# The issue order of all five engines and the buffer of each tile, worked out anew for an adaLN block with Hedgehog linear attention and a channel MLP

## The chip, the cores and the metric

The kernel runs on one core of one Trainium2 chip. The metric is the device time of one execution in microseconds, the median of several runs. The engines are named as in the profile: PE multiplies matrices (PEld loads its weights), DVE is the vector engine, ACT the scalar engine, POOL the GpSimd engine, and SP issues the transfers (DMAs).

## The reference

A residual block on x of 2048 rows by 512, all in fp32, with one condition vector c. Six rows of 512 come out of `silu(c) @ w_mod` and modulate the two halves of the block. Cut to what matters:

```python
mod = (_silu(c) @ w_mod).reshape(c.shape[0], 6, 1, -1)      # sa, ca, ga, sb, cb, gb
h = _layernorm(x) * (1 + ca) + sa
q, k, v = split(h @ wqkv)                                    # 32 heads of 16
pq, pk = q @ w_phi, k @ w_phi                                # per head
phi = concat([softmax(p), softmax(-p)])                      # for pq and for pk, 32 features
kv, z = phi_k^T @ v, sum_s phi_k                             # sums over all 2048 rows
o = (phi_q @ kv) / (phi_q @ z + 1e-6)
x = x + ga * (o @ wo)
h = _layernorm(x) * (1 + cb) + sb
y = gelu(_layernorm(h) @ w1 + b1) @ w2 + b2                  # 512 -> 1376 -> 512
x = x + gb * y
```

The sums `kv` and `z` run over all rows, so nothing of the second half can start before the last row of the first half is through.

## The kernel before, in words

The 2048 rows are cut into eight blocks of 256 rows (two tiles of 128). Every large product is made as three fp32r products of high and low parts (`mm3`), so each operand is split first: ACT copies the high part, and DVE or POOL subtracts to get the low part.

The first half (to about 148 us in the profile) works block by block. PE transposes the normalised rows (`hp`), ACT applies the modulation and rounds (`hf`, `hT`), and PE projects to keys (`pk`), values (`pv`) and queries (`pq`). Each key tile then goes through a chain (`k_chain`): DVE takes maximum and minimum (`mxk`), subtracts twice (`ek`), ACT takes the exponential, DVE sums (`smk`) and inverts (`rck`), POOL multiplies, and DVE adds the result to the running sum (`zps`; the last time into `zb`). PE sums the values weighted by the finished key tiles into `pkv`. Beside this the background work (`bg`) prepares the modulation rows (`wms`) and splits weights (`wo`, `w2a`): load, POOL scales, ACT copies, DVE subtracts. At the very start the weights of keys and queries are folded with `w_phi` on PE (`fold`), and the condition is turned into columns: `wm` is loaded, and DVE and POOL multiply it with `scp`.

The two halves meet in `zp`, a product of PE with `zb`, the sum over all key tiles.

The second half works on blocks 0 to 7 again, one ahead of the other: attention of a later block (`attn_ea`: exponentials `eq`, the denominator `dz`, a rearrangement through DRAM `eb`, `et_dram`, `eT`), then `po` (attention output), `oT` (its split), `pw` (times wo), the layer norms (`la`, `lb`, `lc`), a rearrangement of the result (`y`, `yf`; by transposes `yp` on PE for the first two blocks) into `yT`, and the MLP: eleven products `pg` per block (`up`, "u"), each followed by gelu and a copy on ACT (`g`) and a subtraction on DVE, and eleven pairs of products `py` (`down`, "d") that use them.

None of the order is left to a scheduler. The code above is run once to record every operation in a queue under a part (a block), a name and an engine letter (p PE, a ACT, v DVE, g POOL, s SP), and a list called `ISSUE` then says in which order they are issued. All instructions go through one line of the recorder, so the profile shows L194 for everything:

```python
    def issue(self):
        for n, order in enumerate(ISSUE):
            for name in order.split():
                for f in self.queues[n + name.count("+") - name.count("-"), name.strip("+-")].popleft():
                    f()
```

A token such as `-k0.v` takes the next operation of DVE in the key chain of tile 0 of the block before the one that the row stands for. Each engine executes what is issued to it strictly in that order; between engines semaphores hold back what isn't ready. The second table, `SLOTS`, says for a tag of buffers which one each tile gets, and where a tag has no entry the buffers are taken in turn:

```python
    def slot(tag, bufs):
        n = used[tag] = used.get(tag, -1) + 1
        return f"{tag}_{SLOTS[tag][n] if tag in SLOTS else n % bufs}"
```

A tile that takes a buffer still in use waits for the last reader of the tile before it. The tag `mm` has four PSUM banks, through which nearly all products pass.

## Time and profile before

| | |
|---|---|
| median of 3 runs | 496.57 us (496.22 to 496.67) |
| the profiled execution | 496.27 us, of which the span from first to last instruction is 494.2 us |
| mean granted PE clock | 0.995 |
| PE busy | 475.0 us (96% of the span) |
| DVE, ACT, POOL busy | 349.5, 236.4 and 230.8 us |
| moved | 40.42 MB read, 18.88 MB written |

PE is busy almost throughout, so a reader looks first at the few places where it isn't. A busy PE is not PE at its peak, since its pieces overlap and their ends are modelled. Rows of the profile give start, duration or busy time in us, the engine, the operation, the tile written and the tiles read, and in brackets the idle time before it with what ended it.

### The profile page before, as it was taken

What the parts mean: (1) busy time and instruction counts of PE and PEld (TensorE: products, weight loads), DVE (VectorE), ACT (ScalarE), POOL (GpSimd) and SP (SyncE); (2) the same over time, 40 slices, a digit from 0 to 9 for tenths busy, and PEclk for the clock granted to TensorE, in tenths of its full rate; (3) what the DMA queues carried; (4) which work ended last, traced back from release to release, by engine and by line L of the source; (5) the groups of instructions that cost most, each with busy time, mean ns of one, the idle gap of its engine ahead of it and who ended that gap; (6) DMA issues with size and microseconds to landing.
All of it is one profiled execution on the core that took longest, in us unless ns stands there. A gap on an engine that the chain in (4) does not pass through costs nothing. (4 is left out here: it accounts for less than half of the span.)

```text
span 494.2 us, 8537 instructions
## 1 busy us (share of the span) xinstructions
PE 475.0 (96%) x3311; PEld 403.7 (82%) x3311; DVE 349.5 (71%) x662; ACT 236.4 (48%) x439; POOL 230.8 (47%) x175
## 2 busy tenths in 40 slices
PE   4999999899999998999999999999999999999996
PEld 4887877687877785998897998897898998898985
DVE  5998998998996539986986796793785382462311
ACT  3687764546563344547264633842544324134321
POOL 3467875677794684756474534533452210010000
PEclk9999999999999999999999999999999999999999
DMA  8752556542043716116364544507813443202101
GB/s 271 292 170 87 170 192 193 172 127 86 1 129 122 238 42 193 44 38 214 90 171 127 136 123 126 131 1 229 205 37 87 124 132 86 86 1 85 44 0 44
DMA packets 64760, 59.85 MB, mean 121 GB/s; under 512 B 40256, under 2 KB 52176, under 8 KB 64464
## 3 DMA queue, kind: packets, MB, share of 16 engines
q1 hardware_dynamic: 64720, 59.31, 38.8%
q8 instruction: 26, 0.43, 0.3%
q14 instruction: 14, 0.11, 0.1%
HBM read 40.42 MB, written 18.88 MB: 120 GB/s over the span
## 5 line engine op out<-in xcount | busy, mean ns | idle before, releaser
L194 PEld LDWEIGHTS pg<-yT,w 128*128 128x128 f32 x960 | 121.1, 191 | 6.4 <-DVE yT L194 1.0
L194 PE MATMUL pg<-yT,w 128*128 128x256 f32 x960 | 123.2, 283 | 1.5 <-DVE yT L194 0.8
L194 ACT ACTIVATE pg<-pg,blob 128x256 f32<-128x256 f32 (+1 forms) x88 | 39.2, 445 | 99.5 <-PE pg L194 90.9
L194 PE MATMUL py<-w2a,g 128*128 128x512 f32 x288 | 72.7, 392 | 0.0
L194 DVE TENSOR_TENSOR g<-pg,g 128x256 fp32r<-128x256 f32 x80 | 32.3, 412 | 53.8 <-ACT g L194 53.7
L194 PEld LDWEIGHTS py<-w2a,g 128*128 128x128 f32 x288 | 52.0, 189 | 9.9 <-ACT pg L194 0.4
L194 PE MATMUL pv<-wvh,hT 128*128 128x512 f32 x192 | 48.0, 405 | 2.3 <-ACT hf L194 2.0
L194 PE MATMUL pw<-wo,oT 128*128 128x512 f32 x192 | 48.0, 395 | 1.7 <-DVE oT L194 1.0
L194 PE MATMUL py<-w2b,g 128*128 128x512 f32 x192 | 47.9, 394 | 0.0
L194 ACT ACTIVATE g<-pg 128x256 fp32r<-128x256 f32 x80 | 30.7, 384 | 35.3 <-PE py L194 30.4
L194 PE MATMUL pk<-wk,hT 128*128 128x512 f32 x192 | 46.6, 394 | 0.9 <-ACT vf L194 0.9
L194 PE MATMUL pq<-wq,hT 128*128 128x512 f32 x192 | 46.9, 396 | 0.0
L194 POOL TENSOR_TENSOR ez<-eq,zb 128x1024 f32<-128x1024 f32 x15 | 36.2, 2412 | 21.9 <-DVE dz L194 12.4
L194 POOL TENSOR_TENSOR eq<-eq,rcq 128x1024 f32<-128x1024 f32 x15 | 29.9, 2009 | 33.3 <-DVE rcq L194 33.3
L194 PEld LDWEIGHTS pv<-wvh,hT 128*128 128x128 f32 x192 | 36.5, 194 | 10.6 <-ACT hf L194 2.2
L194 PEld LDWEIGHTS pw<-wo,oT 128*128 128x128 f32 x192 | 35.0, 188 | 11.4 <-DVE oT L194 3.4
L194 PEld LDWEIGHTS pk<-wk,hT 128*128 128x128 f32 x192 | 35.4, 188 | 8.5 <-ACT vf L194 1.3
L194 PEld LDWEIGHTS pq<-wq,hT 128*128 128x128 f32 x192 | 35.4, 188 | 8.5 <-issue 0.5
L194 PEld LDWEIGHTS py<-w2b,g 128*128 128x128 f32 x192 | 34.9, 188 | 7.7 <-issue 1.2
L194 POOL TENSOR_TENSOR ek<-ek,rck 128x1024 f32<-128x1024 f32 x16 | 32.5, 2041 | 7.8 <-DVE rck L194 6.6
L194 POOL TENSOR_TENSOR yT<-yf,yT 128x256 fp32r<-128x256 f32 x12 | 9.0, 767 | 44.3 <-ACT yT L194 44.3
L194 DVE TENSOR_REDUCE dz<-ez 128x64 f32<-128x1024 f32 x16 | 19.2, 1198 | 7.8 <-POOL ez L194 7.8
(146 smaller groups left out, 771.2 us busy)
## 6 DMA issues: line engine op xcount, KB each, us to landing
et_dram<-eb SPq DMA_DIRECT2D x48, 128.0 KB, 2.4
eT<-et_dram SPq DMA_DIRECT2D x12, 512.0 KB, 4.2
xt<-in_x SPq DMA_DIRECT2D x8, 512.0 KB, 4.7
wms<-in_wmodT SPq DMA_DIRECT2D x8, 512.0 KB, 3.9
x<-in_x SPq DMA_DIRECT2D x8, 512.0 KB, 4.0
out<-x SPq DMA_DIRECT2D x16, 256.0 KB, 2.0
pq_dram<-qs SPq DMA_DIRECT2D x6, 512.0 KB, 2.9
pq<-pq_dram SPq DMA_DIRECT2D x6, 512.0 KB, 3.7
```

Source lines behind the costliest of these rows:

```text
L194: return lambda *a, **k: self.later.hold(self.letter, lambda: f(*a, **k))
```

## The change

The recorded operations are the same, each with the same shape, on the same engine: 1816 entries in both lists. What is new are the two tables. `ISSUE` lists the entries in another order for all five engines, with more entries moved over a block's border (`+` and `-` before a name), and `SLOTS` names the buffer for every tile of 43 tags, where before it did so for seven and the rest went in turn. No tag has more or fewer buffers. The first lines of the diff:

```diff
 SLOTS = {
-    "acc": "1010101010101010101",
-    "two": "100101",
-    "ek": "010110101010101010101010",
+    "acc": "1010101101001101001",
+    "two": "010110",
+    "xt": "110101010101010101",
+    "st6a": "10001100",
...
 ISSUE = [
     """
-db.s si.a x0.s dk.s dm.s dm.s dm.s dk.s dk.s -init.v si.v si.v bd.v si.v s0.v s0.v s0.v s0.v s0.v -init.v dk.s
+db.s x0.s dk.s dk.s dm.s dm.s dv.s si.a si.v -init.v si.v si.v dm.s sr.p s0.v s0.v dk.s s0.v dq.s -init.v bd.v sr.a
```

Three places of the new order follow. In the changed file the recorder's line is L226 instead of L194.

The first place is the start of the program on SP, the loads. Before (`k` is a quarter of the key weights, `wm` of the first modulation columns, `xt` rows of x):

```order
L194 DMA blob<-in_small 128x217
L194 DMA xt<-in_x 128x2x512
L194 DMA k<-in_wkT 128x512
L194 DMA wm<-in_wmodT 128x1024 x3
L194 DMA k<-in_wkT 128x512 x3
L194 DMA wm<-in_wmodT 128x1024
L194 DMA wv_s<-in_wv 128x1024
```

And now:

```order
L226 DMA blob<-in_small 128x217
L226 DMA xt<-in_x 128x2x512
L226 DMA k<-in_wkT 128x512 x2
L226 DMA wm<-in_wmodT 128x1024 x2
L226 DMA wv_s<-in_wv 128x1024
L226 DMA wm<-in_wmodT 128x1024
L226 DMA k<-in_wkT 128x512
L226 DMA q<-in_wqT 128x1024
L226 DMA wm<-in_wmodT 128x1024
L226 DMA k<-in_wkT 128x512
```

One piece of `k` moved ahead of the first `wm`; the last two pieces of `k` and the last two of `wm` moved back, behind a load of `wv_s` and, for the last of each, one of `q`.

The second place is the end of the first half, on two engines. On DVE, before (the two instructions that write `zb` end the sum that `zp` waits for):

```order
L194 RECIPROCAL rck<-smk 128x64
L194 TENSOR_TENSOR w2a<-ws,w2a 128x1024
L194 TENSOR_TENSOR zps<-zps,ek 128x512
L194 TENSOR_REDUCE mxk<-pk 128x32 x2
L194 TENSOR_TENSOR ek<-pk,mxk 128x32x16
```

Now, with the end of the sum:

```order
L226 RECIPROCAL rck<-smk 128x64
L226 TENSOR_TENSOR zps<-zps,ek 128x512 x4
L226 TENSOR_TENSOR zb<-zps,ek 128x512 x2
L226 TENSOR_TENSOR w2a<-ws,w2a 128x1024
L226 TENSOR_REDUCE dz<-ez 128x64
```

The last subtraction of `w2a`, which stood fifteen rows ahead of the `zb` row, now stands behind it. On PE, around `zp`, before:

```order
L194 MATMUL pq<-wq,hT_330 128x512
L194 MATMUL pkv<-ek,vf 32x64 x32
L194 MATMUL zp<-zb,ones 128x512 x2
L194 MATMUL pq<-wq,hT_329 128x512 x2
L194 MATMUL pq<-wq,hT_330 128x512
L194 MATMUL pq<-wq,hT_329 128x512 x2
L194 MATMUL pq<-wq,hT_330 128x512
L194 MATMUL pq<-wq,hT_329 128x512 x2
L194 MATMUL pq<-wq,hT_330 128x512
L194 MATMUL pq<-wq,hT_329 128x512 x2
L194 MATMUL pq<-wq,hT_330 128x512
L194 MATMUL pkv<-ek,vf 32x64 x32
```

And now:

```order
L226 MATMUL pq<-wq,hT_330 128x512
L226 MATMUL pkv<-ek,vf 32x64 x64
L226 MATMUL zp<-zb,ones 128x512 x2
L226 MATMUL pq<-wq,hT_329 128x512 x2
L226 MATMUL pq<-wq,hT_330 128x512
```

The 32 `pkv` products that came after `zp` now come before it, in one run with the others.

The third place is on PE at the start of the MLP, where the second block's `pw` (`oT_454` and `oT_455` are its operand's high and low part) and the first block's `yp` and `pg` meet. Before:

```order
L194 MATMUL pw<-wo,oT_454 128x512 x2
L194 MATMUL pw<-wo,oT_455 128x512
L194 MATMUL yp<-blob,h_414 128x128 x8
L194 MATMUL pg<-yT_460,w_359 128x256
L194 MATMUL pg<-yT_461,w_359 128x256
```

And now:

```order
L226 MATMUL yp<-blob,h_414 128x128 x8
L226 MATMUL pw<-wo,oT_454 128x512 x2
L226 MATMUL pw<-wo,oT_455 128x512
L226 MATMUL pw<-wo,oT_454 128x512 x2
L226 MATMUL pw<-wo,oT_455 128x512
L226 MATMUL pw<-wo,oT_454 128x512 x2
L226 MATMUL pw<-wo,oT_455 128x512
L226 MATMUL pw<-wo,oT_454 128x512 x2
L226 MATMUL pw<-wo,oT_455 128x512
L226 MATMUL pg<-yT_460,w_359 128x256
```

Twelve `pw` products now stand between the transposes `yp` and the first `pg`, which reads what ACT and DVE make of `yp`; before, `pg` followed `yp` at once.

## Prediction

> **What bounds the kernel now.** I read the page's first part, then busy time by stage, then the waits of PE and of DVE, and last the order of time around the largest waits. The page:

> ```profile
> span 494.2 us, 8537 instructions
> PE 475.0 (96%) x3311; PEld 403.7 (82%) x3311; DVE 349.5 (71%) x662; ACT 236.4 (48%) x439; POOL 230.8 (47%) x175
> ```

> PE leaves 19.2 us of the span unused. The stages show that DVE's 71% is an average over two different halves (columns: stretch, its length, then busy us and instructions of PE, PEld, DVE, ACT, POOL, then the granted clock, DMA share and GB/s):

> ```profile
> 0.00:12.00 12.00, 5.86 (x24) 5.16 (x24) 5.90 (x21) 4.41 (x8) 3.76 (x8) 1.00 0.81 266
> 12.00:148.00 136.00, 131.08 (x1030) 107.00 (x1030) 128.62 (x224) 86.42 (x144) 97.56 (x64) 0.99 0.45 148
> 148.00:330.00 182.00, 179.43 (x1221) 152.26 (x1222) 138.03 (x253) 88.10 (x158) 99.81 (x74) 1.00 0.41 122
> 330.00:494.20 164.20, 158.65 (x1039) 139.28 (x1037) 76.96 (x167) 57.52 (x131) 29.70 (x31) 1.00 0.30 87
> ```

> From 12 to 148 us DVE is busy for 128.6 of 136 us, nearly as much as PE. From 148 us on PE alone bounds: it is busy for 338.1 of 346.2 us. What ends PE's waits (engine, tile, releaser: us in total, times, longest):

> ```profile
> PE scp L194 <- DVE sc L194: 4.1, 1, 4.1
> PE fold L194 <- DMA k<-in_wkT: 2.2, 2, 1.4
> PE pv L194 <- ACT hf L194: 2.0, 1, 2.0
> PE po L194 <- DMA eT<-et_dram: 1.1, 1, 1.1
> PE pw L194 <- DVE oT L194: 1.0, 4, 0.3
> PE pk L194 <- ACT vf L194: 0.9, 1, 0.9
> PE pg L194 <- DVE yT L194: 0.8, 1, 0.8
> PE zp L194 <- DVE zb L194: 0.7, 1, 0.7
> PE pw L194 <- ACT oT L194: 0.7, 1, 0.7
> ...
> PE pg L194 <- POOL yT L194: 0.4, 1, 0.4
> ...
> PE pg L194 <- ACT yT L194: 0.3, 1, 0.3
> ```

> And DVE's waits between 12 and 148 us:

> ```profile
> DVE mxk L194 <- PE pk L194: 2.9, 3, 1.7
> DVE wo L194 <- ACT wo L194: 2.2, 2, 1.1
> DVE smk L194 <- ACT ek L194: 1.0, 2, 0.7
> DVE w2a L194 <- ACT w2a L194: 0.7, 1, 0.7
> ```

> So the first half ends at `zp`, when DVE has done all it has in front of `zb`, and the second half is PE's work from there plus its waits. The largest waits in order of time, and the work at the end:

> ```profile
> 147.92 1.98 PE L194 MATMUL zp<-zb,ones 128*128 128x512 f32 x4 [0.75 <-DVE zb L194]
> ...
> 152.58 1.10 PE L194 MATMUL pkv<-ek,vf 128*32 128x64 f32 x64
> ...
> 190.80 4.61 PE L194 MATMUL pw<-wo,oT 128*128 128x512 f32 x19 [0.29 <-DVE oT L194]
> 195.24 1.03 PE L194 MATMUL yp<-blob,h 128*128 128x128 f32 x8
> 196.53 0.38 PE L194 MATMUL pg<-yT,w 128*128 128x256 f32 x1 [0.25 <-ACT yT L194]
> 197.70 1.58 PE L194 MATMUL pg<-yT,w 128*128 128x256 f32 x11 [0.79 <-DVE yT L194]
> ...
> 489.64 1.39 DVE L194 TENSOR_TENSOR x<-py,x 128x512 f32<-128x512 f32 x2 [0.79 <-PE py L194]
> ```

> **The change part by part.** The operations are the same, so PE's 475 us of work stay. I sum against the profiled execution's own 496.27 us (span 494.2 and 2.1 around it), which lies 0.3 under the median of 496.57.

> The start. DVE's long run begins when the first `wm` has landed:

> ```profile
> 9.17 0.69 DVE L194 CUSTOM_DVE_ANT_0 prod<-wm,scp 128x512 f32<-128x512 f32 x1 [0.90 <-DMA wm<-in_wmodT]
> ```

> One more quarter of `k` (0.26 MB) is now queued on SP ahead of it. At the 266 GB/s of the first 12 us that is 1.0 us. PE may gain here, since two folds can run at once and the first `pk` comes earlier, but DVE starts its run later. The last `wm` and `k` land later too, each behind `wv_s` (0.52 MB), the last of them also behind `q`; DVE has the `wv_s` subtraction and the other columns to do meanwhile. I take +0.7 us, between 0 (the queue was not the limit) and +1.5.

> DVE's work before `zb`. One subtraction of `w2a` moves behind it, and nothing else crosses. Its row:

> ```profile
> L194 DVE TENSOR_TENSOR w2a<-ws,w2a 128x1024 fp32r<-128x1024 f32 x3 | 3.6, 1199 | 0.7 <-ACT w2a L194 0.7
> ```

> That is 1.2 us, of which about 0.1 overlaps its neighbour: -1.1 us at `zp`. Behind `zp` DVE has room, and the low part of `w2a` is read only by the first `py`, so it costs nothing there; the cover is DVE's 44 idle us between 148 and 330, and without it the 1.1 would stay.

> DVE's waits in the first half: 2.9 + 2.2 + 1.0 + 0.7 = 6.8 us. I added up DVE's work that stands in the order between the second subtraction of `ek` and the `smk` of the same tile, which is what hides the exponential. The smallest such cover in the old order is 1.3 us, and eight of the sixteen are under 1.85; in the new order the smallest is 1.65 and all others are over 2. On the other hand DVE's lead over PE at `mxk` is only a little better, and `w_prep` is spread in the same way. I take a third off, -2.0 us. The ends are -5 (nearly all gone) and +4 (the new order meets waits of its own, over half as many again).

> PE's work behind `zp`. The `pkv` run of 1.10 us (row at 152.58) moves ahead of `zp`, where PE waits for DVE anyway: -1.1 us, between -1.2 and 0, the latter if PE instead of DVE is last at `zp`. The first half also has five `pkv` runs instead of nine, which gives PE a little slack there.

> PE's waits behind `zp`. At the first `pg` the 0.79 and 0.25 us go, because twelve `pw` now stand between; at the pace of the nineteen in 4.61 us, 0.24 each, they make 2.9 us, against the 1.0 that was missing. I take -1.1 with the small slow step beside them. The wait for `eT` (1.1 us) should go as well. In the old list the last of the ten transfers of a block's rearrangement stands 0.7 to 4.9 us of PE's work ahead of the first `po`, in the new one 6.4 to 21.8 (matmuls counted between them, by these rows):

> ```profile
> 352.89 1.43 PE pg L194 x12
> ...
> 379.55 1.02 PE po L194 x32
> ...
> 405.25 0.70 PE py L194 x3
> ```

> The `pw` waits for `oT` within the blocks (0.3 each) had 1.4 to 7.0 us of such cover and now 3.3 to 10.4. Some came in spite of 7.0, so I take only half a microsecond there. The wait after the last `po` before the MLP stays: `pw` follows `po` directly in both orders. Together -2.7, between -3.6 and +1 (as long a wait elsewhere). What is late next is PE itself.

> Gelu and exponentials. ACT changes its function table when it goes from gelu to the exponentials and back:

> ```profile
> 311.94 1.28 ACT L194 ACT_TABLE_LOAD   x1
> 313.23 1.06 ACT L194 ACTIVATE eq<-eq 128x1024 f32<-128x1024 f32 x1
> 314.31 1.28 ACT L194 ACT_TABLE_LOAD   x1
> 315.61 0.45 ACT L194 ACTIVATE pg<-pg,blob 128x256 f32<-128x256 f32 x1
> ```

> The old order has 14 such loads, the new one 18: 4 x 1.28 = 5.1 us more on ACT, which has over 200 idle us behind `zp`. They cost time only where a `py` waits for its gelu. The cover, PE's work between a `pg` group and its first `py`, falls from a median of 7.8 us to 4.9, and three blocks now begin with 1.44 us of it; the old order has five pairs at 1.44 or less and no wait for `g` in PE's list. I take +0.5, between 0 and +5.1 (all four in full). [...]

> The end is as before: the last `py` pair, the two additions, the stores.

> Sum: +0.7 - 1.1 - 2.0 - 1.1 - 2.7 + 0.5 = -5.7; 496.27 - 5.7 = 490.6 us.

> **The rivals.** Half gain: DVE's waits stay at 6.8 and the start costs its full 1.5. Then it is -5.7 + 2.0 + 0.8 = -2.9, or 493.4 us. For it speaks that DVE's lead over PE hardly changes; against it the longer covers of the exponentials. Chance 0.15.

> Slower, by ACT at a block's head: in the new order the second exponential of a pair stands in ACT's queue with a load on either side and the next block's first gelu behind it, and two blocks then leave PE only 1.44 us before the `py`. If POOL delivers `eq` late there, PE stands still for the load, the exponential and the load, 1.28 + 1.06 + 1.28 = 3.6 us. A wait as long as that may cost more than itself:

> ```profile
> 83.65 2.20 PE L194 MATMUL pv<-wvh,hT 128*128 128x512 f32 x9
> ...
> 97.12 4.11 PE L194 MATMUL pv<-wvh,hT 128*128 128x512 f32 x10 [1.99 <-ACT hf L194]
> ```

> After the wait of 1.99 us ten `pv` took 4.11 us where nine took 2.20, that is 1.7 us more. So 3.6 + 1.7 = 5.3 for each of two blocks, 10.6 in all, in place of the +0.5: 490.6 - 0.5 + 10.6 = 500.7 us. It makes the kernel slower from 6.2 us on, the gain without that term. Against it: PE has 5 to 7 us of work between the exponentials' place in the list and the end of that `pg`. Chance 0.12. [...]

> Slower, by DVE: the new order makes DVE wait twice as long in the first half, 13.6 us instead of the 4.8 that I count. That adds 8.8: 499.4 us. It decides from 10.5 us of waits. Only an order that put subtractions of weights ahead of ACT's copies would do it, and those rows (2.2 and 0.7 us) show that it can happen. Chance 0.06.

> No change: what is gained at one wait comes back at the next, since PE is 96% busy and each of its waits is about 1 us. The places that I name have different causes, so this has 0.05, at 496.3 us.

> **How the numbers follow.** The forecast has the remaining 0.62, at 490.6 us, with 486 to 494 as its own range. All lower ends at once would be 0 - 1.1 - 5 - 1.2 - 3.6 + 0 = -10.9, or 485.4, and hardly come together: I set the low end at 486.0. The high end of 497.0 takes in the half gain and no change and leaves out the two slower cases, 0.18. A measurement of this kernel can tell about 0.2%, 1 us, from no change. Faster: 0.62 + 0.15 = 0.77; same 0.05; slower 0.12 + 0.06 = 0.18.

> **What would show it.** Right: `zp` starts about 2.4 us earlier, near 145.5; DVE's waits between 12 us and `zp` are under 6 us; no wait of PE for `eT` or `yT` near the start of the MLP; 18 table loads with no wait of PE for `g`. Wrong: `zp` at or after 148, a `py` behind `g` in PE's list of waits, or new waits behind `zp` of 4 us or more.

## The result, and the profile after

The changed kernel takes 501.42 us (median of 4 runs, 499.36 to 502.32), the kernel before, run beside it, 496.39 us. The ratio is 1.0104, with a 95% interval of 1.0063 to 1.0145: slower by 1%, where I forecast 490.6 us. The profiled execution took 501.69 us. Its page:

```profile
span 499.9 us, 8539 instructions
...
PE 476.7 (95%) x3311; PEld 406.6 (81%) x3311; DVE 366.6 (73%) x662; ACT 243.1 (49%) x443; POOL 229.7 (46%) x175
```

PE does the same 3311 products in nearly the same busy time. DVE does the same 662 instructions and is busy for 17.1 us more (349.5 before). That number is the key to all that follows, though only a part of it costs time. By stage (columns as before):

```profile
0.00:12.00 12.00, 6.57 (x27) 6.01 (x28) 4.50 (x16) 3.83 (x6) 1.95 (x6) 1.00 0.79 256
12.00:148.00 136.00, 131.61 (x1093) 107.75 (x1092) 132.93 (x229) 85.80 (x144) 93.17 (x64) 0.99 0.43 143
148.00:330.00 182.00, 172.46 (x1099) 145.76 (x1098) 142.77 (x237) 89.70 (x156) 103.33 (x73) 0.98 0.44 135
330.00:499.90 169.90, 166.06 (x1097) 147.06 (x1096) 86.36 (x183) 63.75 (x140) 31.26 (x34) 1.00 0.25 75
```

From 12 to 148 us DVE is busy for 132.93 us instead of 128.62, and from 148 to 330 us PE for 172.46 instead of 179.43: the time is lost there. DVE's waits between 12 and 148 us, all that the view lists:

```profile
DVE st6a L226 <- DMA xt<-in_x: 1.5, 1, 1.5
DVE smk L226 <- ACT ek L226: 0.8, 1, 0.8
DVE hf L226 <- ACT prod L226: 0.3, 1, 0.3
```

That is 2.6 us, where 6.8 stood before: the new order does what the forecast said of it, and more. But the 4.2 us that DVE no longer waits are 4.3 us that it is busy longer, and `zp` starts about where it did (147.49 us, before 147.92). PE's waits:

```profile
PE scp L226 <- DVE sc L226: 3.7, 1, 3.7
PE pw L226 <- DVE vec L226: 3.1, 1, 3.1
PE yp L226 <- DVE g L226: 2.8, 1, 2.8
PE hp L226 <- DVE ek L226: 2.2, 1, 2.2
PE qp L226 <- issue: 1.4, 1, 1.4
...
PE pw L226 <- ACT oT L226: 0.7, 1, 0.7
PE py L226 <- ACT g L226: 0.6, 1, 0.6
PE qp L226 <- DVE x L226: 0.5, 1, 0.5
```

The waits for `eT` and `yT` are gone. In their place stand two that no step of mine had, `pw` and `yp`. In order of time:

```profile
193.63 4.14 PE L226 MATMUL pw<-wo,oT 128*128 128x512 f32 x10 [3.13 <-DVE vec L226]
...
230.65 0.66 PE L226 MATMUL yp<-blob,h 128*128 128x128 f32 x4 [2.76 <-DVE g L226]
231.06 5.95 PE L226 MATMUL py<-w2b,g 128*128 128x512 f32 x18
```

Behind each of these two waits PE is slow for a while: ten `pw` took 4.14 us here, and 2.56 us in e13 below; eighteen `py` 5.95 us, and 4.36 in e3. That is 1.6 us more each time. Behind `zp` PE waits 9.6 us in all (with two small ones of 0.3 and 0.2), before 4.3. Three of the waits, 2.2 us together, are of `qp`, PE's transposes of the exponentials `eq`; they stand in every kernel with the new order, and no run touched them.

Which DVE instructions became longer? The groups of DVE, before (busy us, mean ns of one):

```profile
L194 DVE SCALAR_TENSOR_TENSOR nmc<-stc,rsc 128x1 f32<-128x1 f32 x16 | 3.7, 235 | 1.9 <-POOL rsc L194 1.9
...
L194 DVE TENSOR_TENSOR w2b<-ws,w2b 128x1024 fp32r<-128x1024 f32 x2 | 2.5, 1225 | 0.9 <-ACT w2b L194 0.8
...
L194 DVE SCALAR_TENSOR_TENSOR nma<-sta,rsa 128x2 f32<-128x2 f32 x8 | 1.3, 156 | 0.8 <-POOL rsa L194 0.8
```

and after:

```profile
L226 DVE SCALAR_TENSOR_TENSOR nma<-sta,rsa 128x2 f32<-128x2 f32 x8 | 6.4, 797 | 0.8 <-POOL rsa L226 0.8
L226 DVE SCALAR_TENSOR_TENSOR nmc<-stc,rsc 128x1 f32<-128x1 f32 x16 | 5.8, 370 | 3.9 <-POOL rsc L226 3.8
L226 DVE TENSOR_TENSOR w2b<-ws,w2b 128x1024 fp32r<-128x1024 f32 x2 | 5.1, 2536 | 4.3 <-ACT w2b L226 4.3
```

An `nma` handles 2 numbers per partition and takes 156 ns before, 797 after. One of them, on DVE:

```profile
93.40 1.89 DVE L226 SCALAR_TENSOR_TENSOR nma<-sta,rsa 128x2 f32<-128x2 f32 x1
```

and what POOL did then:

```profile
91.84 1.53 POOL L226 TENSOR_TENSOR rsa<-vea,mhalf 128x2 f32<-128x2 f32 x1 [2.16 <-DVE vea L226]
93.34 1.93 POOL L226 TENSOR_TENSOR ek<-ek,rck 128x1024 f32<-128x1024 f32 x1
```

POOL's product ends at 95.27, DVE's `nma` at 95.29. Five of the eight `nma` lasted 0.70 to 1.89 us in this way, the other three 0.15 or 0.16. PE pays for this one: on DVE the two subtractions `ek` stand behind it, and PE's `hp` waits for them:

```profile
97.23 0.63 PE L226 MATMUL hp<-blob,xt 128*128 128x128 f32 x4 [2.24 <-DVE ek L226]
```

The wait of `pw` has the same shape. On DVE, the cast of `glast`, the row that adds a bias, stands ahead of the two subtractions of `oT` that `pw` reads:

```profile
188.80 2.40 DVE L226 CAST glast<-ones 1x256 fp32r<-1x256 f32 x1
...
192.89 0.68 DVE L226 TENSOR_TENSOR oT<-po,oT 128x512 fp32r<-128x512 f32 x1
```

and on POOL at that time:

```profile
188.70 2.36 POOL L226 TENSOR_TENSOR w<-w1s,w 128x1024 fp32r<-128x1024 f32 x1
```

The cast of 256 numbers ends at 191.20, the product at 191.06. The kernel before has such a meeting of the cast too, beside POOL's `eq` from 158.30 to 161.28, but at a place where PE's list shows no wait for anything that stands behind it on DVE:

```profile
159.51 1.92 DVE L194 CAST glast<-ones 1x256 fp32r<-1x256 f32 x1
```

So my theory: **a DVE instruction that reads SBUF in a certain way is held while a POOL instruction runs, and the new order puts more such pairs side by side, or ahead of work that PE waits for**. The rival: the order of DVE's own queue makes the waits, whatever POOL does.

### The profile page after: what moved, and what is told of

It is laid out like the page before. It is cut to its first block, busy times and chain, and to the rows that moved or that the text cites. A ratio compares the mean times of both kernels' runs of the same rounds, so it can differ in the third digit from the quotient of the medians.

```text
span 499.9 us, 8539 instructions
## 1 busy us (share of the span) xinstructions
PE 476.7 (95%) x3311; PEld 406.6 (81%) x3311; DVE 366.6 (73%) x662; ACT 243.1 (49%) x443; POOL 229.7 (46%) x175
## 4 chain that ended last, share of the span: by engine, by line
PE 49%; DMA 2%; DVE 2%; ACT 1%; POOL 0%; issue 0%; SPq 0%
PE py L226 22%; PE pg L226 21%; PE pw L226 5%; PE po L226 1%; DMA yf<-yt_dram 1%; DMA yt_dram<-yb 1%; DVE mxq L226 0%; DVE eb L226 0%; DVE nmc L226 0%; DVE x L226 0%; ACT L226 0%; POOL eq L226 0%; SPq L226 0%; ACT eq L226 0%; ACT pg L226 0%
## 5 line engine op out<-in xcount | busy, mean ns | idle before, releaser
L226 PEld LDWEIGHTS pg<-yT,w 128*128 128x128 f32 x960 | 122.9, 191 | 5.1 <-DVE g L226 0.3
L226 PE MATMUL pg<-yT,w 128*128 128x256 f32 x960 | 124.5, 283 | 0.0
L226 ACT ACTIVATE pg<-pg,blob 128x256 f32<-128x256 f32 (+1 forms) x88 | 39.2, 445 | 114.2 <-PE pg L226 100.9
L226 PE MATMUL py<-w2a,g 128*128 128x512 f32 x288 | 73.4, 393 | 0.6 <-ACT g L226 0.6
L226 DVE TENSOR_TENSOR g<-pg,g 128x256 fp32r<-128x256 f32 x80 | 33.1, 415 | 50.8 <-ACT g L226 50.4
L226 PEld LDWEIGHTS py<-w2a,g 128*128 128x128 f32 x288 | 51.6, 189 | 10.2 <-ACT g L226 0.8
L226 PE MATMUL pw<-wo,oT 128*128 128x512 f32 x192 | 48.1, 402 | 3.9 <-DVE vec L226 3.1
L226 PE MATMUL py<-w2b,g 128*128 128x512 f32 x192 | 50.5, 405 | 0.0
L226 PE MATMUL pv<-wvh,hT 128*128 128x512 f32 x192 | 48.2, 405 | 1.1 <-DVE ek L226 0.9
L226 PE MATMUL pk<-wk,hT 128*128 128x512 f32 x192 | 47.5, 396 | 1.0 <-ACT hT L226 1.0
L226 POOL TENSOR_TENSOR ez<-eq,zb 128x1024 f32<-128x1024 f32 x15 | 37.0, 2469 | 23.5 <-DVE dz L226 16.4
L226 PEld LDWEIGHTS pw<-wo,oT 128*128 128x128 f32 x192 | 36.8, 194 | 12.5 <-DVE vec L226 3.6
L226 PE MATMUL pq<-wq,hT 128*128 128x512 f32 x192 | 46.2, 395 | 0.0
L226 PEld LDWEIGHTS pv<-wvh,hT 128*128 128x128 f32 x192 | 36.5, 194 | 9.6 <-DVE ek L226 1.3
L226 PEld LDWEIGHTS pq<-wq,hT 128*128 128x128 f32 x192 | 35.6, 188 | 8.5 <-issue 0.9
L226 PEld LDWEIGHTS py<-w2b,g 128*128 128x128 f32 x192 | 35.6, 194 | 8.2 <-issue 1.6
L226 PEld LDWEIGHTS pk<-wk,hT 128*128 128x128 f32 x192 | 35.1, 188 | 8.6 <-ACT hT L226 1.3
L226 POOL TENSOR_TENSOR eq<-eq,rcq 128x1024 f32<-128x1024 f32 x15 | 28.9, 1938 | 20.8 <-DVE rcq L226 20.5
L226 POOL TENSOR_TENSOR ek<-ek,rck 128x1024 f32<-128x1024 f32 x16 | 31.0, 1942 | 14.8 <-DVE rck L226 14.7
L226 ACT ACTIVATE g<-pg 128x256 fp32r<-128x256 f32 x80 | 30.5, 382 | 12.8 <-PE py L226 9.2
L226 POOL TENSOR_TENSOR rsb<-veb,mhalf 128x1 f32<-128x1 f32 x16 | 8.8, 555 | 57.6 <-DVE veb L226 57.6
L226 DVE TENSOR_REDUCE dz<-ez 128x64 f32<-128x1024 f32 x16 | 19.4, 1212 | 12.0 <-POOL ez L226 11.9
```

The costliest lines, as they stand in the source:

```text
L226: return lambda *a, **k: self.later.hold(self.letter, lambda: f(*a, **k))
```

## The experiments

**e1: eight kinds of DVE instruction alone and beside POOL.** A kernel of its own, which computes nothing of the block: each kind runs twice alone and then twice beside products of 128x1024 on POOL.

> Computes none of the block: it copies x to the output and runs eight kinds of DVE instruction, first alone and then beside twelve POOL products of 128x1024 (about 2 us each in the rows of the changed kernel). Theory one (DVE is held while POOL works): an instruction with two operands in SBUF lasts up to 2 us longer beside POOL than alone, whatever its size; those with one operand in PSUM and reductions last as long as alone, within 5%. Theory two (the longer DVE instructions of the changed kernel come from something else, such as waits counted as work): no kind lasts more than 10% longer beside POOL.

The rows alone and beside (the first of each of four kinds, and of the small one the second, since POOL had not begun at the first):

```profile
4.24 0.68 DVE L45 TENSOR_TENSOR twobigalone<-a,b 128x512 f32<-128x512 f32 x1
...
6.89 0.42 DVE L49 COPY copyalone<-a 128x512 f32<-128x512 f32 x1
...
7.69 0.10 DVE L43 SCALAR_TENSOR_TENSOR twosmallagain<-a,b 128x2 f32<-128x2 f32 x1
...
11.84 0.68 DVE L44 TENSOR_TENSOR psumonebeside<-pa,b 128x512 f32<-128x512 f32 x1
12.44 2.54 DVE L45 TENSOR_TENSOR twobigbeside<-a,b 128x512 f32<-128x512 f32 x1
...
17.99 1.96 DVE L49 COPY copybeside<-a 128x512 f32<-128x512 f32 x1
...
20.33 1.83 DVE L43 SCALAR_TENSOR_TENSOR twosmallbesides<-a,b 128x2 f32<-128x2 f32 x1
```

Two SBUF operands: 0.10 to 1.83 us and 0.68 to 2.54. One SBUF operand, fp32: a copy 0.42 to 1.96, an addition of a constant 0.42 to 1.43; these two theory one didn't have. Untouched, alone and beside: an operand in PSUM (0.68), a reduction (1.21), a reciprocal (0.55 and 0.54). So the holding is real, and its price is not a factor: 1.73 us more on the instruction of 0.10, 1.86 on the one of 0.68. In the changed kernel it is what is left of POOL's instruction: the `nma` of 93.40 ends 0.02 us after POOL's product, the cast 0.14.

**e2 to e5: DVE's and ACT's order behind `zp`.** Each moves entries of the changed kernel's list. e2 moves the cast behind the work that `pw` waits for; e3 moves a gelu copy and its subtraction, for which `yp` waits, ahead of a reduction and two rearrangements; e4 is both; e5 also moves ACT's copy of the second `yT` ahead of an exponential:

```diff
@@ e2 @@
-o10.p t11.a mp.v w1.g lp.s
+o10.p t11.a w1.g lp.s
...
-la0.v u.v la0.v -mp.v la0.g
+la0.v u.v la0.v -mp.v -mp.v la0.g
@@ e3 @@
-lc0.a +a.v a.s u.a u.p
+lc0.a u.a u.v +a.v a.s u.p
...
-+a.g y.p u.v u.a d.p
++a.g y.p u.a d.p
@@ e5 @@
-a.s d.p +a.a d.p +a.g y.a d.p
+a.s d.p y.a +a.a d.p +a.g d.p
```

> The changed kernel with one DVE instruction moved: the cast into glast (2.40 us beside a POOL product, at 188.8 us) goes from ahead of the two oT subtractions to where its partner stands, in block 0 of the second half. If the order of DVE's queue at that place makes PE wait, the wait of pw (3.1 us) shrinks by about 2.4 and the slow pw after it (ten at 0.41 us instead of 0.23) are at full pace: 2.4 + 1.9 = 4.3 us less, near 497.3 us against 501.5. If pw waits for something else, or the time comes back at the next wait, 500.5 us or more.

e2: 497.83 us, ratio 1.0038 [1.0019, 1.0058]; the wait of `pw` is 1.2 us instead of 3.1. The time is near the 497.3 that was expected, though the ten `pw` behind the wait still take 4.14 us in the profiled execution.

> The changed kernel with one DVE instruction moved: the subtraction of g for the ninth pg of block 0 (at 230.2 us) goes ahead of two transposes and one mxq reduction, three places earlier. If PE's yp at 230.65 waits for a PSUM bank that this subtraction sets free, the 2.8 us of wait shrink to about 0.5 and the ten slow py behind it are at full pace: 2.3 + 1.9 = 4.2 us less, near 497.3 us. If the bank is not the reason, no change.

e3: 500.48 us, ratio 1.0097 [1.0062, 1.0131]: a miss. The wait of `yp` falls to 0.4 us, and this comes instead:

```profile
234.49 3.14 PE L226 MATMUL pg<-yT,w 128*128 128x256 f32 x24 [2.13 <-DVE yT L226]
```

> Both moves of the two kernels before in one. If the two places are independent, the gains add: about 8.5 us less than the changed kernel, near 493 us, which is under the kernel before (496.4). If what is won at the first place is lost at the second, near 497 us.

e4: 497.64 us, ratio 1.0044 [1.0021, 1.0067], no better than e2 alone: a miss.

> Both moves of the run before, and a third: on ACT, the copy of the second yT of block 0 goes ahead of the exponential and its table load, behind which it stands in the changed kernel (226.98 us, while its yp was ready before 223.8). If the gain of the earlier g subtraction was lost at this next wait (pg for yT, 2.1 us, and 24 pg in 4.63 us behind it instead of 2.87), this gives 2.1 + 1.7 = 3.8 us less than both moves alone, near 493.8 us. If the time is lost in the first half or later in any case, no change from 497.6.

e5: 497.75 us, ratio 1.0038 [1.0016, 1.0060]: a miss too. The wait for `yT` is 2.2 us still, since on DVE its subtraction stands behind a reduction that waits for the exponential:

```profile
226.93 1.22 DVE L226 TENSOR_REDUCE smq<-eq 128x64 f32<-128x1024 f32 x1 [1.84 <-ACT eq L226]
228.06 0.68 DVE L226 TENSOR_TENSOR yT<-yp,yT 128x512 fp32r<-128x512 f32 x1
```

Of the two new waits, then, `yp` isn't worth its size: there the next thing was late as well. The cast is.

**e6 and e7: `nma` on POOL.** In e6 the `nma` of blocks 1 to 7 is two short instructions of POOL, so DVE has none to be held there; e7 does the same to the kernel before:

```diff
-        nm = ln_neg(st, rs, 2, "a")
+        if b:
+            nm = stile([2], "nma")
+            nc.gpsimd.tensor_tensor(nm, st[:, :, 0], rs, op=OP.mult)
+            nc.gpsimd.tensor_tensor(nm, mzero, nm, op=OP.subtract)
+        else:
+            nm = ln_neg(st, rs, 2, "a")
```

> The changed kernel with seven of the eight nma instructions (two operands in SBUF, 0.8 us each on average there, 0.16 in the kernel before) replaced by two small POOL instructions each, behind the POOL instruction that gives their operand. If being held by POOL makes DVE slow in the first half, DVE's work before zb falls by about 5 us and zp comes 2 to 4 us earlier (PE then bounds it): 498 to 499.5 us against 501.4. If the first half is bound by PE, or POOL's added work (about 1.1 us each) costs as much, no change.

> The same replacement in the kernel before, as a control. Its nma take 0.16 us each, so by the theory that POOL holds DVE there is nothing to gain: within 1 us of the kernel before, on the slower side if anything, by POOL's added work. If nma on POOL is better in itself, this gains as much as in the changed kernel.

e6: 498.28 us, ratio 1.0049 [1.0028, 1.0071], 3.1 us less than the changed kernel (2.7 by the ratios). e7: 495.54 us, ratio 0.9995 [0.9974, 1.0017]: nothing. The seven little instructions cost something in the new order alone. `zp` in e6:

```profile
141.23 1.98 PE L226 MATMUL zp<-zb,ones 128*128 128x512 f32 x4
```

That is 6.3 us earlier than in the changed kernel's execution, and 4.9 earlier than the mean of the seven kernels that share its first half (146.1). About 3 of them arrive at the end.

> The three moves and nma on POOL together. If the places and the first half add: 493.8 - 2.5, near 491.3 us, 1% under the kernel before. If they overlap, 493 to 495.

e8, e5 and e6 together: 495.71 us, ratio 1.0009 [0.9988, 1.0030]; equal to before, but above the 493 to 495 that I had set as its upper case.

**e9, e10 and e12: more of the places behind `zp`.** e9 is e5 with the subtraction of `yT` ahead of the reduction, and the copies and subtractions of `oT` earlier; e10 adds e6's `nma`; e12 adds to e10 the chain of the last MLP weights (`wlast`) ahead of the next block's differences and exponential:

```diff
@@ e9 @@
-o11.p lb01.v o10.a lb01.v o11.a lc00.v o10.v lc00.a lb01.v o11.v w11.p
+o11.p o10.a o11.a o10.v o11.v lb01.v lb01.v lc00.v lc00.a lb01.v w11.p
...
-+a.g d.p +a.v -w2.g +lp.s +a.a d.p a.s y.v d.p
++a.g d.p y.v +a.v -w2.g +lp.s +a.a d.p a.s d.p
@@ e12 @@
-a.v a.s +a.g y.p
+a.v a.s -w2.g +a.g y.p
...
-y.a +a.a d.p +a.g d.p y.v +a.v -w2.g +lp.s
+y.a -w2.a +a.a d.p +a.g d.p y.v -w2.v +a.v +lp.s
...
-a.s +a.g -w2.a u.v
+a.s +a.g u.v
...
-u.p a.v --w2.v u.p
+u.p a.v u.p
```

> The changed kernel with the three moves of e5 and two more on DVE: the subtraction of yT ahead of the reduction smq, which waits for an exponential, and the two subtractions of oT ahead of one operation of the layer norm. Theory (each PE wait behind zp is a place in DVE's queue where a ready product stands behind something that isn't needed or isn't ready): the wait of pg for yT (2.2 us in e5) goes and the wait of pw falls below 0.5 us; with the slow stretch behind the first the time is 493 to 495.5 us. Rival (what is taken from one wait comes back at the next one, as in e3 to e5): 497 to 498.5 us.

> The five moves of e9 and the small operations nma of the key chain's layer norm on POOL, as in e8. Theory: zp near 142 and 350 us or less behind it, 491 to 493.5 us, less than both kernels. Rival: equal to e8, 495 to 496.5 us, since time won at zp comes back as waits behind it.

> The kernel of e10 with one more chain moved: the last of the second MLP weights (POOL's scaling of ws, ACT's copy and DVE's subtraction into wlast) ahead of the four POOL differences and the exponential of the next block, behind which it stands in e10. Theory (PE's waits behind zp are places where a ready piece stands behind work that waits): the two waits of py for wlast (1.7 and 0.3 us in e10) go, 492 to 493.5 us, less than both kernels. Rival (won time comes back as the next wait): 494.5 to 495.5 us.

e9: 496.86 us, ratio 1.0026 [1.0008, 1.0044]; e10: 494.92 us, 0.9988 [0.9968, 1.0008]; e12: 494.49 us, 0.9975 [0.9957, 0.9993]. Each is above the range of its theory, by 1.0 to 1.4 us, and within 0.2 us of its rival's. In e9 and e10 the wait for `yT` goes and one of 1.7 us for `wlast` comes; in e12 that goes, and these stand there:

```profile
PE po L226 <- DMA eT<-et_dram: 1.8, 1, 1.8
...
PE pg L226 <- DVE g L226: 1.2, 1, 1.2
...
PE py L226 <- DVE g L226: 0.7, 1, 0.7
```

So the waits mostly move on. Those behind `zp` sum to 9.6 us in the changed kernel, 7.6 in e2, 7.3 in e4, 7.9 in e5, 6.9 in e9, 8.5 in e10 and 8.4 in e12: the move of the cast takes off what it removes, and of the others most comes back as another wait. e12 is the one version whose interval lies under the kernel before, by a quarter of a per cent.

**e13: POOL's product moved, DVE's order untouched.** This separates the two theories at `pw`. In the changed kernel the entry `w1.g` moves from row 7 to row 8, behind five other POOL operations:

```diff
-o10.p t11.a mp.v w1.g lp.s
+o10.p t11.a mp.v lp.s
...
-u.p a.g la0.v a.v -w1.g lp.s
+u.p a.g la0.v a.v -w1.g -w1.g lp.s
```

> The changed kernel with one POOL entry moved and nothing on DVE: the product w that runs beside the cast of glast at 188.70 us stands behind the four differences eq. Theory one (the cast is long only because POOL's product runs beside it): the cast takes 0.2 to 0.4 us instead of 2.4, the wait of pw falls from 3.1 to about 1 us, 497.3 to 499 us, as with the cast itself moved in e2. Theory two (the cast is long by itself, or the wait is made by the order in DVE's queue alone): cast 1.9 to 2.4 us, wait 3.1 us, 500.5 to 502 us.

e13: 498.28 us, ratio 1.0056 [1.0036, 1.0077]. On DVE and on PE:

```profile
188.48 0.29 DVE L226 CAST glast<-ones 1x256 fp32r<-1x256 f32 x1
```

```profile
191.20 2.56 PE L226 MATMUL pw<-wo,oT 128*128 128x512 f32 x10 [1.01 <-DVE vec L226]
```

Theory one: the cast takes 0.29 us at the very place where it took 2.40, the wait falls to 1.0, and 3.1 us (2.4 by the ratios) are won without a move on DVE. No slow stretch follows, but the profiled execution has none at all before its last microsecond (mean clock 0.999; the other seven 0.988 to 0.995), so this run alone doesn't say what the stretches cost.

**e11, e14 and e15: the cast put into the kernel before.** The names in the list take whatever is next in their queue, and for e11 I overlooked that: the entry that came to stand ahead of `oT` was the other of the two of `glast`, a subtraction of 0.42 us. In e15, likewise, the POOL entry that moved to the place was `wlast` (1.01 us), not `w`.

```diff
@@ e11 @@
-q1.a a0.g mp.v kf.v
+q1.a a0.g kf.v
...
-o11.p o10.a o10.v o11.a
+o11.p o10.a mp.v o10.v o11.a
@@ e14 @@
-q1.a a0.g mp.v kf.v
+q1.a a0.g kf.v
...
-a1.v a1.v mp.v a1.v la00.v
+a1.v a1.v a1.v la00.v
...
-o11.a lb01.v o11.v lc00.v
+o11.a lb01.v mp.v o11.v lc00.v
...
-w11.p lb01.g +la1.v
+w11.p lb01.g mp.v +la1.v
@@ e15, on top of e14 @@
-q4.p t10.p w1.g la00.g
+q4.p t10.p la00.g
...
-o11.v lc00.v w2.g lp.s
+o11.v lc00.v w1.g w2.g lp.s
```

> The kernel before with one entry moved: the cast of glast on DVE stands directly ahead of the first subtraction of oT in the second block, as in the changed kernel. Theory: oT comes 1.9 to 2.4 us later and PE waits there for about as long, with or without a slow stretch behind it: 1.5 to 4 us more than before, 498 to 500 us. Rival (DVE's order there doesn't matter and the wait has another cause): no change, 496 to 496.8 us.

e11: 495.44 us, ratio 1.0002 [0.9983, 1.0020], which says no more than that 0.4 us are free there.

> The kernel before with the cast of glast on DVE moved directly ahead of the second subtraction of oT in the second block (and its own subtraction behind it), where no POOL product runs: POOL's ws starts 0.5 us later. Theory one: the cast takes 0.3 to 0.5 us and PE waits at most 0.4 us longer, 495.5 to 497 us. Theory two: the cast takes 1.9 us as at its old place, PE waits as much longer, 497.5 to 500 us.

> As e14, and POOL's product w, which ended at 181.7 us, moved so that it starts at about the same moment as the cast. Theory one: the cast takes about 2.4 us, the wait of pw for oT grows from 0.3 to about 2.3 us, and the slow stretch of PE may add 1.4 to 1.9: 497.5 to 500 us. Theory two: as in e14.

e14: 498.15 us, ratio 1.0044 [1.0024, 1.0065]; e15: 498.57 us, 1.0057 [1.0038, 1.0076]. Theory one's number for e14 failed, because a product did run there. The rows of e11 have it already: POOL's `ws` runs from 188.03 to 190.41 us, and the second subtraction of `oT` starts at 188.74. On DVE and on POOL in e14:

```profile
190.08 1.71 DVE L188 CAST glast<-ones 1x256 fp32r<-1x256 f32 x1
```

```profile
189.28 2.37 POOL L188 TENSOR_TENSOR ws<-ws,gbb 128x1024 f32<-128x1024 f32 x1 [0.69 <-ACT oT L188]
```

```profile
192.57 6.20 PE L188 MATMUL pw<-wo,oT 128*128 128x512 f32 x19 [2.16 <-DVE oT L188]
```

The cast ends at 191.79, the product at 191.65. One instruction of 0.29 us beside a product thus costs the kernel before 2.2 to 2.8 us (0.44 and 0.57% of 495.7): 1.9 of waiting and 1.6 of slow `pw` (19 in 6.20 us, 4.61 before), less 0.5 by which the next wait, of `pg` for `yT`, is shorter (0.34 instead of 0.79). e15 has the same product beside it, so the two don't differ in that.

**e16: both meetings taken out.** `nma` on POOL as in e6 and POOL's `w` late as in e13; nothing else of DVE moves.

> The changed kernel with DVE's order as it is but for the removed nma: POOL's product w stands later (as in e13) and the nma of the key chains runs on POOL (as in e6). So only two meetings of DVE with a POOL product are taken out. Theory one (these meetings are the whole loss against the kernel before, and their prices add): 501.4 - 3.1 - 3.1 = 495.2, between 494.5 and 496.2 us. Theory two (the order of the queues costs something beside them, or one gain is lost behind the other): 497 to 498.5 us.

e16: 494.88 us, ratio 0.9989 [0.9969, 1.0009]. In parts of the time before: the changed kernel +1.04%, e6 +0.49, e13 +0.56, e16 -0.11. Singly the two take off 0.55 and 0.48 points, together 1.15. Within the intervals (0.2 points each way, 0.4 for the changed kernel) the prices add, and together they are as large as the whole loss.

## Why the prediction was wrong

**What bounds.** Right for PE behind `zp`, and half right for DVE in front of it. At `zp` itself PE now comes last: in all twelve profiles of the block with the new order the first `zb` ends 0.4 to 0.8 us before `zp` starts. Between 14.5 us and `zp` PE stands still for 2.2 to 4.9 us in the seven of them with `nma` on DVE, and for 0.2 to 1.3 us in the five others, so there PE bounds the first half.

**The step that failed** stands ahead of all terms: "The operations are the same, so PE's 475 us of work stay." I held that for DVE too and took each duration from the old order. DVE's work is 366.6 us instead of 349.5, for the same instructions, because a duration on DVE depends on what POOL does at that moment (an `nma` took 0.15 or 0.16 us in three places, 0.70 to 1.89 in five). Two parts of this cost time: the `nma` ahead of `zp` (5.1 us more), and the cast, only 0.5 us longer than before but now ahead of `oT`. Others don't show in the time: e16 leaves `w2b` (2.6 us more) and `nmc` (2.1 us more) as they are and is as fast as the kernel before. By e16 the two meetings are worth 1.15%, 5.7 us of the 10.8 between the forecast and the result; the rest lies in PE's waits behind `zp`, below. None of the rivals has DVE held by POOL; the forecast of a slower kernel at 0.18 rested on other mechanisms, which did not come.

**The start, +0.7 (0 to +1.5).** Right in the mean. DVE's first `prod` starts at 9.16 to 10.96 us in the twelve profiles with the new order, mean 9.87, and at 8.88 to 9.17 in the five with the old one, mean 9.00. The changed kernel's own, 10.96, is the latest.

**DVE's waits, -2.0 (-5 to +4).** The waits fell by 4.2 us, twice what I took. It bought next to nothing, since five of the eight `nma` were held and took 5.1 us more. Where the `nma` are off DVE (e6, e8, e10, e12, e16) `zp` starts at 141.2 to 142.9 us, mean 142.0; in the seven other kernels with the new first half at 144.5 to 147.5, mean 146.1; in the five with the old one at 146.5 to 147.9, mean 147.5. So the new first half is worth 5.5 us without these meetings, and 1.4 with them, where I had 2.4 for start, `w2a` and waits.

**PE's waits behind `zp`, -2.7 (-3.6 to +1).** Each wait that I named went. But new ones brought the sum from 4.3 to 9.6, +5.3, and two slow stretches added 3.2, far outside my end of +1. This is the second step that failed, "What is late next is PE itself": I had counted PE's cover for the waits that existed and not looked, on DVE, for what stands ahead of each thing that PE will want. Of the wait of 3.1 at `pw`, 2.1 are a meeting with POOL (1.0 is left in e13); the one of 2.8 at `yp` is a matter of order, but when it goes, the next one takes its place (e3).

**`pkv`, -1.1 (-1.2 to 0).** The move came as said, one run of 1.99 us ahead of `zp` and none behind. Its condition, that PE waits for DVE at `zp` anyway, didn't hold: PE's list has no wait for `zb` any more, and the run ends where `zp` begins. So the 1.1 us that left the second half stand in front of it, and the term is about 0, the end that I had given for this case. Behind `zp` the sum is +5.3 + 3.2 - 1.1 = +7.4, and 6.1 were measured (352.4 against 346.3 us from `zp` to the end).

**Gelu and table loads, +0.5.** Right in size: 18 loads of 1.28 us each, 23.1 in all where the 14 before took 18.0, and one wait of `py` for `g`, 0.6 us. The rival at ACT's block heads, 10.6 us, did not come. By my own test a `py` behind `g` was to count as wrong; it is the size that I had in the sum. The third sign that I had named, new waits behind `zp` of 4 us or more, came as well.

**What stays open.** Without the two meetings (e16) the kernel is as fast as before, not 5.7 us faster, although `zp` comes about 5.5 us earlier. In the profiled execution of e16 the way from `zp` to the end takes 352.4 us, 6.1 more than before, and most of this is found: PE's waits sum to 8.0 us instead of 4.3, of which `yp` (2.8) and `qp` (2.2) are the largest new ones, slow stretches behind `pw` and `yp` take 3.3 us, and `pkv` gives 1.1 back. That execution, 496.21 us, is 1.3 us above the median of e16, so a part of it is chance. What `qp` waits for was not tried. Nor was one of the two new tables tried without the other, so no run says what the buffers of `SLOTS` do by themselves.

## What to carry to other kernels

Before a reordering is priced, list each DVE instruction with two SBUF operands, and each fp32 copy, cast or addition of a constant from SBUF, against what POOL runs at that moment in the new order: here a tiny one beside a long POOL product took what was left of the product (an `nma` of 0.16 us up to 1.89, the cast of 0.29 us 2.40), and that costs time if something that PE waits for stands behind it. Put such small work where POOL is idle (the cast of e13, 0.29 us) or on POOL itself (e6, 3.1 us less than the changed kernel), or give it a PSUM operand (0.68 us alone and beside POOL in e1; not tried in the block); or shift the POOL product if the DVE order is good, which here was worth about as much as moving the cast (0.48 and 0.66 per cent of the time). When a wait is removed from a full queue, expect most of it back at the next piece (7.6 us of waits behind `zp` in e2, 8.4 in e12 with more of them taken out), and look at that piece before counting the gain.

## What the hardware showed unexpectedly

A one-operand fp32 copy from SBUF is held by POOL about as much as a subtraction of two tensors (0.42 to 1.96 us in e1, 0.29 to 2.40 for the cast; the subtraction 0.68 to 2.54). POOL took longer beside DVE too: its `rsa`, at 0.70 us in the median of eight, took 1.53 (row at 91.84 above) beside DVE's subtraction of `wo`, which ran from 91.60 to 92.82. And PE's slow stretch doesn't depend on the length of the wait alone. In e13 eighteen `py` ran at full pace behind the wait of 2.76 us at `yp`, which in the changed kernel made them 1.6 us longer; in e16 ten `pw` were slow behind a wait of 1.01 us, though in e13 they were not:

```profile
227.08 4.34 PE L226 MATMUL py<-w2b,g 128*128 128x512 f32 x18
```

```profile
186.05 3.82 PE L226 MATMUL pw<-wo,oT 128*128 128x512 f32 x10 [1.01 <-DVE vec L226]
```

```profile
190.39:193.80 3.41, 0.28 (x2) 0.17 (x2) 3.31 (x8) 0.74 (x1) 0.75 (x2) 1.00 0.04 8
193.80:197.21 3.41, 3.41 (x9) 2.64 (x10) 2.84 (x4) 0.88 (x2) 1.86 (x3) 0.50 0.00 0
```

The wait at `yp` lies within one such stretch there (227.93 to 231.34, PE busy for 0.69 us) and is followed by half the clock. In e13 it falls across two, each with more work in it, and the clock stays:

```profile
221.52:224.94 3.42, 2.22 (x15) 1.52 (x13) 3.42 (x5) 2.65 (x6) 0.12 (x1) 1.00 0.01 1
224.94:228.35 3.41, 1.68 (x10) 1.47 (x11) 2.61 (x6) 1.67 (x2) 2.50 (x3) 1.00 0.86 219
```

When the seventeen traces of the block are cut into such stretches, from their first full clock on, half the clock follows each of the 25 with PE busy for 1.53 us or less, and none with more than 1.84; of the 16 between, it follows six. The changed kernel's drops, at 98.23, 193.80 and 231.34 us, lie 28 and 11 times 3.41 us apart. The stretch ahead of e16's slow `pw` has PE busy for 1.75 us.
